# Pooled attention and two expert layers on one core: respacing the attention of the first batch and moving the probability-times-v product in the middle stage

## The chip, the cores and the metric

One core of one Trainium2 chip runs the whole program in one launch. The metric is device time in microseconds (us) for one execution, taken as the median of several. The engines named below are TensorE (PE, the matrix unit), VectorE (DVE), ScalarE (ACT), GpSimd (POOL) and SyncE (SP), whose queue issues nearly all transfers here. Each engine works through its own queue strictly in order, and the queues wait for one another through semaphores.

## The reference

q, k and v have the shape 8 batches x 8 heads x 576 positions x 64. The keys and values are averaged over groups of eight positions, so that there are 72 keys per head. The attention output, as 4608 tokens x 512, goes through two dense layers in turn. The weights come as 64-bit floats.

```python
k_p = k.reshape(B, H, Sp, pool, D).mean(axis=3)
v_p = v.reshape(B, H, Sp, pool, D).mean(axis=3)
scores = scale * np.matmul(q, k_p.transpose(0, 1, 3, 2))
scores = scores - np.max(scores, axis=-1, keepdims=True)
attn = np.exp(scores)
attn = attn / (np.sum(attn, axis=-1, keepdims=True) + 1e-09)
attn_out = np.matmul(attn, v_p)              # then to 4608 x 512 tokens: x
x = ((x @ w1) * (x @ w2) @ w3) @ w_out       # 512 -> 1024 -> 1024 -> 512
h = x @ w_in                                 # 512 -> 2048
out = (h * (1.0 / (1.0 + np.exp(-1.702 * h)))) @ w_out2   # 2048 -> 512
```

## The kernel before, in words

**Number format.** Each float32 operand is kept as a high part and a low part, and a product is three matmuls: high by high, high by low, low by high (`mm3`, L114 to L116). `split` makes the two parts: ACT casts the high part (L104), DVE or POOL subtracts for the low part (L105).

**Weight conversion.** `Conv.step` turns one 512 KB tile of 64-bit weights into float32: two ACT passes (L166, L168), a DVE shift (L169) and a POOL addition (L172). A tile then moves along a line of three places. One step later its `turn` runs (only tiles of w3 have one: four PE transposes, L508), and another step later its `done` runs, mostly a `split`. Within one step the source has the new tile first, then the `turn` of the middle one, then the `done` of the old one. Up to nine tiles are loaded ahead.

**Three stages.** First there are 28 conversion steps (the loop at L568). They convert w_out and w3, and `w3_mm` multiplies the two together into `wp_s` as their parts become ready. From the fifth step on each step also calls `tick()`, which advances the attention. Second comes the middle stage (the loop at L602): nine blocks of 512 tokens, each with eight values of f. For every f there are 24 matmuls for x @ w1 and x @ w2, the elementwise product (L641), and `x2_step`, 12 matmuls with `wp_s`; two calls of `tick()` and, while weights are left, two conversion steps go with it. In the last two blocks the weights of the second layer are converted. Third comes the second layer (from L672), which reads its weights back from device memory.

**Attention.** The work is cut into 32 groups, each one batch and two heads. Steps g0 to g6 of a group: g0 transposes k and q on DVE and pools k; g1 makes the scores on PE and subtracts the maximum on DVE; g2 is the exponential on ACT; g3 divides by the sums on DVE. `g_va` and `g_vb` pool v on POOL and split it into `vm` and `vt`. g4 turns the probabilities and splits them into `ph` and `pt`: for the first four groups (the first batch) the turning is done by PE transposes and ACT copies within g4, for the others by 20 DVE transposes at the end of g3 (L314). g6 multiplies with v on PE (L380 to L383), and ACT and DVE write the result into the token block (L390, L391). Most of these tiles exist once, so a step of one group often waits for the group before it.

**Order.** `tick_first` has the first batch, with a group started every two ticks; `tick` has the other groups, one in four ticks s = 0 to 3. Each block of 512 tokens needs four groups: block 0 needs groups 0 to 3, block 1 needs up to group 7. The source order is not the order on the engines. The compiler's scheduler (`schedule_with_timeline_sim=True`) plays the program through with its own time estimates, and an engine takes, of the instructions that are ready in that play, the one that stands first in the source. The queues are then fixed, and on the chip they run in that order whatever the real durations are.

Of the kernel before, what the change touches and what calls it, by code (L numbers as in the profile page):

```python
# [8 lines left out]
F32R = mybir.dt.float32r  # L9
# [3 lines left out]
ALU = mybir.AluOpType  # L13
# [4 lines left out]
P = 128  # L18
T = 512
# [3 lines left out]
def pooled_attention_moe_moe2(  # L23
# [18 lines left out]
    nc = tc.nc  # L42
    B, H, S, D = q.shape
# [11 lines left out]
    NG = B * HP  # L55
    NPE = HP
# [43 lines left out]
    def f32(ap):  # L100
        return ap.bitcast(F32)
# [22 lines left out]
    def sl(i, n=P):  # L124
        return slice(i * n, (i + 1) * n)

    class Conv:
# [26 lines left out]

        def step(self):

            new = None
            if self.staged:
                t, turn, done = self.staged.pop(0)
                lo_w, hi_w = t[:, :, 0], t[:, :, 1]  # L160
                w = cv_p[0].tile([P, T], F32, name="cv", tag="cv", bufs=4)
                wu = w.bitcast(U32)

                e = self.ps[self.n % len(self.ps)] if self.ps else w
                self.n += 1
                nc.scalar.activation(  # L166
                    e, hi_w.bitcast(F32), AF.Prelu, scale=2.0 ** -112, alpha=-2.0 ** 32)
                nc.scalar.activation(lo_w.bitcast(I32), lo_w, AF.Copy, scale=2.0 ** -29)  # L168
                nc.vector.tensor_scalar(  # L169
                    out=wu, in0=e.bitcast(U32), scalar1=3, scalar2=None,  # L170
                    op0=ALU.logical_shift_left)
                nc.gpsimd.tensor_tensor(  # L172
                    out=w.bitcast(I32), in0=w.bitcast(I32), in1=lo_w.bitcast(I32), op=ALU.add)
                give(t)
                new = [w, turn, done]
            mid, old = self.line
            if mid and mid[1]:
                mid[0] = mid[1](mid[0])
            key = old[2](old[0]) if old else None
            self.line = [new, mid]  # L180
            self.load()
            return key
# [8 lines left out]
    with pa_ctx:  # L191
        pa = pa_ctx.enter_context(tc.tile_pool(name="pa", bufs=1))
# [6 lines left out]
            out=mask[:, 0], in_=mask[:, 0], compare_op=ALU.is_gt, fill=0.0,  # L199
            base=SK, pattern=[[0, D]], channel_multiplier=-1)  # L200
        nc.gpsimd.affine_select(
            out=mask[:, 1], in_=mask[:, 1], compare_op=ALU.is_ge, fill=0.0,
# [8 lines left out]
        for t in s_ts:  # L211
# [3 lines left out]
        ident = pa.tile([P, P], F32, name="ident")  # L215
        nc.gpsimd.memset(ident, 1.0)
        nc.gpsimd.affine_select(
            out=ident, in_=ident, compare_op=ALU.is_equal, fill=0.0,
# [6 lines left out]
        g_q, g_k, g_v, g_s = {}, {}, {}, {}  # L225
# [38 lines left out]
        def banks_of(n):  # L264
            return acc[2:] if n < NPE and n % 2 else wk[2:]

        def s_of(n):
            return s_ts[n % 2 if n < NPE else 0]
# [67 lines left out]
        def g_vb(n):  # L336
            vf, vtf = g_v.pop(n)
            nc.scalar.copy(vm[:, 0], vf)
            nc.gpsimd.tensor_tensor(out=vm[:, 1], in0=vf, in1=f32(vm[:, 0]), op=ALU.subtract)
            nc.scalar.copy(vt[:32, D:], vtf)  # L340
            nc.scalar.copy(vt[64:96, D:], vtf)
            nc.gpsimd.tensor_tensor(
                out=vt[32:64, D:], in0=vtf, in1=f32(vt[:32, D:]), op=ALU.subtract)

        def g4(n):
            p0, p1 = g_s.pop(n)
            if n < NPE:
                ps, s_t = banks_of(n), s_of(n)
                p0f, p1f = (t.rearrange("p t c -> p (t c)") for t in (p0, p1))
                for tt in range(4):  # L350
                    nc.tensor.transpose(ps[0][:, sl(tt)], s_t[:, tt, :P], ident)
                nc.scalar.copy(p0f[:, :T], ps[0])
                w = S - T
                nc.tensor.transpose(ps[1][:, :w], s_t[:w, 4, :P], ident[:w, :w])
                for tt in range(3):
                    nc.tensor.transpose(
                        ps[1][:32, w + tt * P:w + (tt + 1) * P], s_t[:, tt, P:], ident)
                nc.scalar.copy(p0f[:, T:S], ps[1][:, :w])
                nc.scalar.copy(p1f[:, :3 * P], ps[1][:32, w:w + 3 * P])
                nc.tensor.transpose(ps[0][:32, :P], s_t[:, 3, P:], ident)  # L360
                nc.tensor.transpose(ps[0][:32, P:P + w], s_t[:w, 4, P:], ident[:w, :w])
                nc.scalar.copy(p1f[:, 3 * P:S], ps[0][:32, :P + w])
            ph = pa.tile([P, 2, S], F32R, name="ph", tag="ph")
            pt = pa.tile([96, S], F32R, name="pt", tag="pt")
            g_s[n] = (ph, pt)
            s0 = p0.rearrange("p t c -> p (t c)")[:, :S]
            s1 = p1.rearrange("p t c -> p (t c)")[:, :S]
            nc.scalar.copy(ph[:, 0], s0)  # L368
            nc.gpsimd.tensor_tensor(out=ph[:, 1], in0=s0, in1=f32(ph[:, 0]), op=ALU.subtract)  # L369
            nc.scalar.copy(pt[:32], s1)  # L370
            nc.scalar.copy(pt[32:64], s1)
            nc.gpsimd.tensor_tensor(out=pt[64:96], in0=s1, in1=f32(pt[:32]), op=ALU.subtract)

        def g6(n):
            b, hp = divmod(n, HP)
# [29 lines left out]
        def tick_first():  # L405

            t = tick_n[0]
            tick_n[0] += 1
            for n in range(NPE):
                if t == 2 * n + 6:  # L410
                    g6(n)
            for n in range(NPE):
                s = t - 2 * n
                if s == 0 and n == 0:
                    g0(0)
                elif s == 1:
                    g1(n)
                elif s == 2:
                    g2(n)
                    g0(n + 1)  # L420
                elif s == 3:
                    g3(n)
                elif s == 4:
                    g4(n)
                    g_va(n)
                elif s == 5:
                    g_vb(n)
            if t == 2 * NPE + 4:
                tick_n[0] = 4 * NPE
                give(s_sl)  # L430

        def tick():
            t = tick_n[0]
            if t < 4 * NPE:
                return tick_first()
            tick_n[0] += 1
            n, s = divmod(t, 4)
            if s == 0:
                if NPE <= n - 1 < NG:
                    g4(n - 1)  # L440
            elif s == 1:
                if n < NG:
                    g1(n)
            elif s == 2:
                if NPE <= n - 1 < NG:
                    g6(n - 1)
                if n < NG:
                    g2(n)
                    g_va(n)
                if n + 1 < NG:  # L450
                    g0(n + 1)
            elif n < NG:
                g3(n)
                g_vb(n)

        wo_s, wp_s, w1_s, w2_s = {}, {}, {}, {}

# [110 lines left out]
        for i in range(n3 + 4):  # L568
            key = conv.step()
# [32 lines left out]
        for blk in range(NB):  # L602
            x = [x_slot(blk, c) for c in range(KM)]
            if blk == NB - 2:

                pa_ctx.close()
                pa = pa_ctx.enter_context(tc.tile_pool(name="pc", bufs=1, reuse_waits="tile"))
# [521 lines left out]
```

## Time and profile before

| what | value |
|---|---|
| median of 3 runs | 1477.35 us (1476.22 to 1478.56) |
| the profiled execution's own time | 1479.71 us |
| its span | 1478.0 us |
| PE busy | 1438.7 us (97%) |
| DVE / ACT / POOL busy | 988.7 / 693.9 / 489.0 us |
| first 28 conversion steps and first batch | about 0 to 113 us |
| middle stage (nine blocks) | about 113 to 730 us |
| second layer | from there to the end |

The shares of busy time are averages over the whole span. The change concerns the first 113 us and the attention of the middle stage, so those stretches have to be read by themselves. A row of a timeline gives the start, the duration, the engine and the line in the kernel, and in square brackets the idle time of that engine just before it and what ended it.

### The profile page before, as it was taken

The numbers are of one execution on the slowest core, as the hardware profiler recorded it, in microseconds if no ns is written. First come the engines' busy times: TensorE is split into PE (matmuls) and PEld (weight loads), VectorE is DVE, ScalarE is ACT, GpSimd is POOL, SyncE is SP. The second block draws the span as 40 slices with busy tenths as digits, with TensorE's granted clock in tenths as the row PEclk, the third lists the DMA queues.
The fourth block names the chain that finished last, engine by engine and source line by source line (L and its number), as shares of the span: only waits on it lengthen the run. The fifth ranks groups of instructions, "written<-read, shape, count | busy, mean of one in ns | idle before, by whom it ended". The sixth has DMA issues, their size and how long they took to land.

```text
span 1478.0 us, 19436 instructions
## 1 busy us (share of the span) xinstructions
PE 1438.7 (97%) x6536; PEld 1190.0 (81%) x6536; DVE 988.7 (67%) x1728; ACT 693.9 (47%) x1212; POOL 489.0 (33%) x589
## 2 busy tenths in 40 slices
PE   6979999999999999999999999999999999999998
PEld 4867888888888888888788887888788888888886
DVE  7888998878787877654737255683559354944554
ACT  7875444434343433366635344552455244534442
POOL 8789656554545555366733100000000000000000
PEclk9989999999999999999999999999999999999999
DMA  9992233323232311199879978877677766785665
GB/s 265 248 233 48 57 85 57 80 46 78 49 77 49 77 33 37 42 325 344 309 236 398 325 243 276 294 211 221 194 244 224 221 197 221 239 234 180 194 213 139
DMA packets 294436, 267.64 MB, mean 181 GB/s; under 512 B 201664, under 2 KB 226240, under 8 KB 294336
## 3 DMA queue, kind: packets, MB, share of 16 engines
q1 hardware_dynamic: 291648, 265.09, 59.8%
q10 hardware_dynamic: 2688, 1.31, 0.3%
q8 instruction: 52, 0.85, 0.2%
q14 instruction: 48, 0.39, 0.1%
HBM read 209.72 MB, written 56.62 MB: 180 GB/s over the span
## 4 chain that ended last, share of the span: by engine, by line
PE 82%; DMA 7%; DVE 5%; ACT 2%; SPq 2%; issue 1%; POOL 1%; DVEq 0%; ACTq 0%; POOLq 0%
PE bk L709 39%; PE wk L114 8%; PE wk L115 8%; PE wk L116 8%; PE acc L114 4%; PE acc L115 4%; PE acc L116 4%; PE wk L277 2%; DMA wud<-wt 2%; DVE p L314 1%; SPq L229 1%; DMA st<-wind 1%; PE bk L115 1%; PE bk L116 1%; PE bk L114 1%
## 5 line engine op out<-in xcount | busy, mean ns | idle before, releaser
L709 PE MATMUL bk<-mv,st 128*128 128x512 f32 x1152 | 272.6, 391 | 0.7 <-DMA st<-wud 0.7
L709 PE MATMUL bk<-xM,st 128*128 128x512 f32 x1092 | 259.0, 390 | 3.9 <-DMA st<-wind 3.7
L709 PEld LDWEIGHTS bk<-mv,st 128*128 128x128 f32 x1152 | 217.3, 189 | 46.3 <-issue 1.1
L709 PEld LDWEIGHTS bk<-xM,st 128*128 128x128 f32 x1092 | 204.5, 188 | 48.6 <-issue 2.5
L114 PE MATMUL wk<-s,s 128*128 128x512 f32 x576 | 227.0, 396 | 2.8 <-DVE a L641 1.2
L116 PE MATMUL wk<-s,s 128*128 128x512 f32 x576 | 224.9, 391 | 2.1 <-DVE s L105 2.1
L115 PE MATMUL wk<-s,s 128*128 128x512 f32 x576 | 224.9, 391 | 0.0
L314 DVE STREAM_TRANSPOSE p<-s_t 32x160 f32<-32x160 f32 (+1 forms) x560 | 178.5, 319 | 10.3
L114 PE MATMUL acc<-s,s 128*128 128x512 f32 x352 | 134.8, 406 | 8.2 <-ACT s L104 3.2
L115 PE MATMUL acc<-s,s 128*128 128x512 f32 x352 | 141.4, 402 | 0.9 <-POOL s L105 0.8
L116 PE MATMUL acc<-s,s 128*128 128x512 f32 x352 | 140.4, 399 | 0.0
L114 PEld LDWEIGHTS wk<-s,s 128*128 128x128 f32 x576 | 108.5, 189 | 26.2 <-DVE a L641 2.1
L116 PEld LDWEIGHTS wk<-s,s 128*128 128x128 f32 x576 | 108.3, 188 | 24.8 <-DVE s L105 2.3
L115 PEld LDWEIGHTS wk<-s,s 128*128 128x128 f32 x576 | 108.4, 188 | 22.1 <-DVE s L391 0.4
L105 DVE TENSOR_TENSOR mv<-g,mv 128x1024 fp32r<-128x1024 f32 x80 | 97.8, 1222 | 33.6 <-ACT mv L104 32.2
L104 ACT CAST mv<-g 128x1024 fp32r<-128x1024 f32 x80 | 84.3, 1054 | 71.8 <-PE bk L709 71.4
L172 POOL TENSOR_TENSOR cv<-cv,s 128x512 int32<-128x512 int32 x72 | 97.5, 1364 | 28.6 <-DVE cv L169 21.1
L105 POOL TENSOR_TENSOR s<-a,s 128x512 fp32r<-128x512 f32 x56 | 72.5, 1294 | 82.5 <-ACT s L104 62.7
L638 ACT COPY a<-wk 128x512 f32<-128x512 f32 x72 | 42.1, 585 | 110.5 <-PE wk L116 89.7
L369 POOL TENSOR_TENSOR ph<-p,ph 128x576 fp32r<-128x576 f32 x32 | 45.7, 1429 | 126.5 <-ACT ph L368 123.9
L114 PEld LDWEIGHTS acc<-s,s 128*128 128x128 f32 x352 | 67.8, 193 | 23.4 <-ACT s L104 5.2
L115 PEld LDWEIGHTS acc<-s,s 128*128 128x128 f32 x352 | 68.2, 194 | 15.0 <-POOL s L105 2.0
(190 smaller groups left out, 2357.9 us busy)
## 6 DMA issues: line engine op xcount, KB each, us to landing
st<-wud SPq DMA_DIRECT2D x96, 512.0 KB, 4.4
st<-wind SPq DMA_DIRECT2D x66, 512.0 KB, 4.7
st<-wind SPq DMA_DIRECT2D x76, 256.0 KB, 3.9
s<-in_moe_w_dram SPq DMA_DIRECT2D x32, 512.0 KB, 6.4
wind<-s SPq DMA_DIRECT2D x32, 512.0 KB, 5.4
s<-in_moe_w_out_dram SPq DMA_DIRECT2D x24, 512.0 KB, 6.5
kr<-in_k_dram SPq DMA_DIRECT2D x128, 72.0 KB, 2.6
qr<-in_q_dram SPq DMA_DIRECT2D x128, 72.0 KB, 2.6
```

Of the source, the lines that this page charges most:

```text
L104: nc.scalar.copy(dst[:, 0], src)
L105: lo_eng.tensor_tensor(out=dst[:, 1], in0=src, in1=f32(dst[:, 0]), op=ALU.subtract)
L114: nc.tensor.matmul(o, a[:, 0, a_sl], b[:, 0, b_sl], start=first, stop=False)
L115: nc.tensor.matmul(o, a[:, 0, a_sl], b[:, 1, b_sl], start=False, stop=False)
L116: nc.tensor.matmul(o, a[:, 1, a_sl], b[:, 0, b_sl], start=False, stop=last)
L172: nc.gpsimd.tensor_tensor(out=w.bitcast(I32), in0=w.bitcast(I32), in1=lo_w.bitcast(I32), op=ALU.add)
L229: nc.sync.dma_start(dst[32 * c:32 * c + 32], src[b, 2 * hp + c // 2, :, 32 * (c % 2):32 * (c % 2) + 32].rearrange("(g t) d -> t g d", t=32))
L277: nc.tensor.matmul(sc[half][:, i * KW:(i + 1) * KW], qT[:, sl(tt)], mov, start=True, stop=True)
L314: nc.vector.transpose(out=dst[:, :nt, 32 * c:32 * c + 32], in_=s_t[32 * c:32 * c + 32, :nt, 32 * r:32 * r + 32])
L369: nc.gpsimd.tensor_tensor(out=ph[:, 1], in0=s0, in1=f32(ph[:, 0]), op=ALU.subtract)
L638: nc.scalar.copy(a, pa_)
L709: nc.tensor.matmul(o, w[:, x, m], b[:, y], start=first and n == 0, stop=last and n == 2, skip_group_check=True)
```

## The change

It has three parts. In `Conv.step` the `done` of the old tile comes first, then the `turn` of the middle one, then the new tile. In the first batch a group starts every three ticks in place of two, and g4 is cut in two: `g4a` (the main turns and the split into `ph`) at the place of g4, and `g4b` (the last two turns and the split into `pt`) one tick later, beside `g_vb`; g6 stays at the sixth tick of its group. Four groups thus end at tick 15 in place of tick 12, and group 4 follows at ticks 16 to 19 as before, which are three conversion steps later. Within the split into `pt` the POOL subtraction is issued before the second ACT copy. In the middle stage g4 moves from s = 0 to s = 1 (just ahead of the next group's g1), and g6 from s = 2 to s = 3 (just ahead of the next group's g3). No instruction is added or taken away.

```diff
         def step(self):
+            mid, old = self.line
+            key = old[2](old[0]) if old else None
+            if mid and mid[1]:
+                mid[0] = mid[1](mid[0])
             new = None
             if self.staged:
...
                 give(t)
                 new = [w, turn, done]
-            mid, old = self.line
-            if mid and mid[1]:
-                mid[0] = mid[1](mid[0])
-            key = old[2](old[0]) if old else None
...
+        def tail_split(n, ph):
+            pt = pa.tile([96, S], F32R, name="pt", tag="pt")
+            s1 = flat(n)[1]
             nc.scalar.copy(pt[:32], s1)
+            nc.gpsimd.tensor_tensor(out=pt[64:96], in0=s1, in1=f32(pt[:32]), op=ALU.subtract)
             nc.scalar.copy(pt[32:64], s1)
-            nc.gpsimd.tensor_tensor(out=pt[64:96], in0=s1, in1=f32(pt[:32]), op=ALU.subtract)
+            g_s[n] = (ph, pt)
...
             for n in range(NPE):
-                if t == 2 * n + 6:
+                if t == 3 * n + 6:
                     g6(n)
             for n in range(NPE):
-                s = t - 2 * n
+                s = t - 3 * n
...
                 elif s == 4:
-                    g4(n)
+                    g4a(n)
                     g_va(n)
                 elif s == 5:
+                    g4b(n)
                     g_vb(n)
-            if t == 2 * NPE + 4:
+            if t == 3 * NPE + 3:
                 tick_n[0] = 4 * NPE
                 give(s_sl)
...
-            if s == 0:
+            if s == 1:
                 if NPE <= n - 1 < NG:
                     g4(n - 1)
-            elif s == 1:
                 if n < NG:
                     g1(n)
             elif s == 2:
-                if NPE <= n - 1 < NG:
-                    g6(n - 1)
...
-            elif n < NG:
-                g3(n)
-                g_vb(n)
+            elif s == 3:
+                if NPE <= n - 1 < NG:
+                    g6(n - 1)
+                if n < NG:
+                    g3(n)
+                    g_vb(n)
```

## Rows read from the trace of the kernel before

**Rows 1.** Windows: length, then each engine's busy us (instructions), granted PE clock, DMA.
```profile
core 0: us, PE busy (x) PEld busy (x) DVE busy (x) ACT busy (x) POOL busy (x), PEclk, DMA share, GB/s
42.00:74.50 32.50, 32.27 (x177) 26.56 (x178) 26.80 (x48) 27.83 (x59) 23.14 (x24) 1.00 0.90 246
74.50:113.50 39.00, 30.48 (x130) 23.69 (x128) 32.82 (x49) 31.33 (x68) 34.11 (x41) 0.87 1.07 226
113.50:190.00 76.50, 74.06 (x351) 61.71 (x352) 67.86 (x154) 35.83 (x80) 59.30 (x79) 1.00 0.26 52
190.00:600.00 410.00, 410.00 (x1978) 346.69 (x1977) 335.43 (x826) 160.72 (x366) 216.27 (x312) 1.00 0.27 59
```

**Rows 2.** Timeline of PE, 74 to 116 us: waits, and matmuls at either clock.
```profile
81.47 0.76 PE L114 MATMUL acc<-s,s 128*128 128x512 f32 x1 [2.84 <-ACT ph L368]
...
107.79 0.50 PE L116 MATMUL wk<-s,s 128*128 128x512 f32 x1 [2.06 <-DVE s L105]
...
108.66 0.63 PE L116 MATMUL wk<-s,s 128*128 128x512 f32 x1
109.08 0.63 PE L114 MATMUL wk<-s,s 128*128 128x512 f32 x1
...
114.91 0.40 PE L114 MATMUL wk<-s,s 128*128 128x512 f32 x1
115.15 0.39 PE L115 MATMUL wk<-s,s 128*128 128x512 f32 x1
```

**Rows 3.** Timeline of PE: first products with v of groups 0, 2 and 3.
```profile
57.72 0.38 PE L380 MATMUL wk<-ph,vm 128*128 128x288 f32 x1
...
87.95 0.52 PE L380 MATMUL wk<-ph,vm 128*128 128x288 f32 x2
...
103.08 0.39 PE L380 MATMUL acc<-ph,vm 128*128 128x288 f32 x1
```

**Rows 4.** Groups by line, POOL up to 57.7 us: count | busy us, mean ns.
```profile
L172 POOL TENSOR_TENSOR cv<-cv,s 128x512 int32<-128x512 int32 x21 | 28.4, 1357 | 9.3 <-DMA s<-in_moe_w_dram 3.3 <-DVE cv L169 3.0 <-issue 0.8
```

**Rows 5.** The same, POOL up to 103.1 us.
```profile
L172 POOL TENSOR_TENSOR cv<-cv,s 128x512 int32<-128x512 int32 x31 | 41.4, 1339 | 10.2 <-DMA s<-in_moe_w_dram 3.3 <-DVE cv L169 3.0 <-issue 1.3
```

**Rows 6.** Timeline of POOL, 99 to 105 us, ahead of the product of group 3.
```profile
99.12 1.43 POOL L372 TENSOR_TENSOR pt<-p,pt 32x576 fp32r<-32x576 f32 x1
100.63 0.79 POOL L329 TENSOR_TENSOR vf<-va,mask 128x128 f32<-128x128 f32 x1
...
102.98 1.28 POOL L105 TENSOR_TENSOR s<-cv,s 128x512 fp32r<-128x512 f32 x1
104.23 0.45 POOL L339 TENSOR_TENSOR vm<-vf,vm 128x128 fp32r<-128x128 f32 x1
```

**Rows 7.** Groups by line, DVE and ACT up to 113.5 us.
```profile
L169 DVE TENSOR_SCALAR cv<-cv 128x512 uint32<-128x512 uint32 x34 | 31.9, 951 | 7.8 <-ACT cv L166 7.5
...
L168 ACT ACTIVATE s<-s 128x512 int32<-128x512 uint32 x40 | 26.9, 678 | 3.5 <-DMA s<-in_moe_w_dram 3.3
```

**Rows 8.** Timeline of DVE, 101 to 112 us.
```profile
107.05 0.68 DVE L105 TENSOR_TENSOR s<-cv,s 128x512 fp32r<-128x512 f32 x1
...
108.68 1.50 DVE L169 TENSOR_SCALAR cv<-cv 128x512 uint32<-128x512 uint32 x2
...
111.17 0.34 DVE L391 TENSOR_TENSOR s<-acc,s 128x224 fp32r<-128x224 f32 x1
```

**Rows 9.** Timeline of PE in the second layer: its longest wait.
```profile
912.79 1.40 PE L709 MATMUL bk<-xM,st 128*128 128x512 f32 x5 [1.79 <-DMA st<-wind]
```

**Rows 10.** Timeline of DVE and PE at the start of block 1.
```profile
187.77 0.78 DVE L255 STREAM_TRANSPOSE kT<-kr 128x576 f32<-128x576 f32 x1
...
189.69 0.73 PE L114 MATMUL wk<-s,s 128*128 128x512 f32 x2 [1.17 <-ACT s L390]
```

**Rows 11.** Timeline of PE at the start of block 2.
```profile
255.83 0.30 PE L383 MATMUL wk<-pt,vt 96*128 96x288 f32 x1
...
260.73 0.62 PE L114 MATMUL wk<-s,s 128*128 128x512 f32 x2
```

More of the change, by code (lines that the diff above doesn't have):

```diff
@@ L343, in g_vb, with flat @@
                 out=vt[32:64, D:], in0=vtf, in1=f32(vt[:32, D:]), op=ALU.subtract)
[L345 to L362, printed above, removed]
+        def flat(n):
+            return [t.rearrange("p t c -> p (t c)")[:, :S] for t in g_s[n][:2]]
@@ L363, in g4, with main_split @@
+        def main_split(n):
             ph = pa.tile([P, 2, S], F32R, name="ph", tag="ph")
[L364 to L367, printed above, removed]
+            s0 = flat(n)[0]
             nc.scalar.copy(ph[:, 0], s0)
             nc.gpsimd.tensor_tensor(out=ph[:, 1], in0=s0, in1=f32(ph[:, 0]), op=ALU.subtract)
+            return ph
+        def tail_split(n, ph):
+            pt = pa.tile([96, S], F32R, name="pt", tag="pt")
+            s1 = flat(n)[1]
@@ L370, in g4, with g4a @@
             nc.scalar.copy(pt[:32], s1)
+            nc.gpsimd.tensor_tensor(out=pt[64:96], in0=s1, in1=f32(pt[:32]), op=ALU.subtract)
             nc.scalar.copy(pt[32:64], s1)
-            nc.gpsimd.tensor_tensor(out=pt[64:96], in0=s1, in1=f32(pt[:32]), op=ALU.subtract)
+            g_s[n] = (ph, pt)
+        def g4a(n):
+            ps, s_t = banks_of(n), s_of(n)
+            p0f, p1f = flat(n)
+            for tt in range(4):
+                nc.tensor.transpose(ps[0][:, sl(tt)], s_t[:, tt, :P], ident)
+            w = S - T
+            nc.tensor.transpose(ps[1][:, :w], s_t[:w, 4, :P], ident[:w, :w])
+            for tt in range(3):
+                nc.tensor.transpose(
+                    ps[1][:32, w + tt * P:w + (tt + 1) * P], s_t[:, tt, P:], ident)
+            nc.scalar.copy(p0f[:, :T], ps[0])
+            nc.scalar.copy(p0f[:, T:S], ps[1][:, :w])
+            nc.scalar.copy(p1f[:, :3 * P], ps[1][:32, w:w + 3 * P])
+            g_s[n] += (main_split(n),)
@@ L374, in g6, with g4b, g4 @@
+        def g4b(n):
+            ps, s_t = banks_of(n), s_of(n)
+            p1f, w = flat(n)[1], S - T
+            nc.tensor.transpose(ps[0][:32, :P], s_t[:, 3, P:], ident)
+            nc.tensor.transpose(ps[0][:32, P:P + w], s_t[:w, 4, P:], ident[:w, :w])
+            nc.scalar.copy(p1f[:, 3 * P:S], ps[0][:32, :P + w])
+            tail_split(n, g_s[n][2])
+        def g4(n):
+            tail_split(n, main_split(n))
         def g6(n):
```

## The prediction, written before the result was known

> **What bounds the kernel now.** I read the windows first, stretch by stretch. From 190 to 600 us PE is busy for all 410.00 us [rows 1]: there the matmuls bound the kernel, and since the change adds and removes none, it can win nothing in that stretch. From 42.0 to 74.5 us PE is also full, 32.27 of 32.50 us. Then, from 74.5 to 113.5 us, it is busy for only 30.48 of 39.00 us at a granted clock of 0.87, and from 113.5 to 190 us for 74.06 of 76.50 us. So the time that this change can reach is the idle time of PE before 190 us: 8.52 us in the starved stretch, 2.44 us after it, and what the lower clock costs.
>
> The timeline of PE shows what ends those waits. The longest one, 2.84 us, ends at 81.47 us, and the matmul behind it belongs to the product of w3 and w_out; the one of 2.06 us ends at 107.79 us with a low part on DVE, and the matmul behind it belongs to block 0 [rows 2]. After such waits the matmuls start 0.42 us apart (108.66 to 109.08) in place of 0.24 us (114.91 to 115.15): PE has gone from 2.4 to 1.2 GHz, and each matmul costs nearly double until it is back.
>
> The timeline then tells who is late. The product with v of group 0 runs at 57.72 us, that of group 2 at 87.95 and that of group 3 at 103.08 [rows 3]. These stand in the source at ticks 6, 10 and 12, which are the conversion steps 10, 14 and 16 (the first tick is in step 4). But POOL has finished 21 conversions by 57.7 us [rows 4] and 31 by 103.1 us [rows 5]. So attention runs 11 and then 15 steps behind its place in the source. The conversions run ahead, the w3 product they feed fills PE until 74.5 us, and then PE has little left but to wait for attention and for the first weights of block 0.
>
> **The change part by part.** *A group per three steps.* The place of group 3's product moves from step 16 to step 19. Nothing is added, so the price is only that of a later place. The scheduler prefers what stands earlier in the source among what is ready, and when group 3's product runs, 31 conversions are done; at step 19 it is still older than everything it competes with. So I cost the shift at nothing. From both sides: three steps at 103.1 / 31 = 3.3 us are 10 us if attention really waited for its place; a gain of as much as the idle 8.5 us if the new spacing made attention and conversions mesh. The row nearest to it, the lag of 15 steps against a shift of 3, says zero. The loads of k and q are issued by g0 on SP's queue and those of v by `g_va`; they move with their groups past the weight loads of at most three steps, and since they wait for a free tile and not for their place, I cost that at nothing too, within the same two ends.
>
> *Last turns and the split into pt a step later, POOL first.* For group 3 POOL ran the subtraction for pt (L372, 1.43 us, at 99.12) directly ahead of vf (L329, at 100.63), and vf leads over the ACT cast to vm at 104.23 [rows 6], which the product needed. In the new order `g_va` stands ahead of that subtraction. It is still needed before the product ends, but the chain over vf, ACT and vm is the longer one, so 1.43 us come off it: -1.4 us on the end of group 3. Bounds: nothing, if the queue order stays, and 1.43 + 1.28 = 2.7 us, if the conversion's low part at 102.98 also moves out of the way.
>
> *The old tile first in a conversion step.* A split no longer stands behind the next but one tile's two ACT passes (0.678 us each [rows 7]) and its DVE shift (0.951 us). A split that contends can come up to 0.68 + 0.68 + 0.95 = 2.3 us earlier. That bears on the low part that ended the wait of 2.06 us at 107.79, computed on DVE at 107.05 [rows 8], so I take the whole wait off: -2.1 us; the lowest end is that none of it goes, since the new tile was then perhaps not ready anyway. The wait at 81.47 may shrink as well, but its matmuls belong to the w3 product, which is done before block 0 can start: that gain becomes later idle time, at zero. The stretch at the lower clock behind 107.79 goes with the wait: five matmuls at 0.18 us extra, -0.9 us. What is late next is the low part of group 3's tokens, L391 at 111.17; it stands behind two shifts (1.50 us together at 108.68), which are younger work too, and it gains the 1.4 us from above. The two gains are in series only in part: block 0 needs the weights first and group 3's tokens last. I count the wait and its clock in full and half of group 3's 1.4 us: -2.1 - 0.9 - 0.7 = -3.7 us at the start of block 0. For the conversions after 600 us I cost the new order at nothing: in the second layer PE's longest wait is 1.79 us, for a transfer [rows 9], and PE's own work covers the rest; if that cover is gone, about 2 us either way.
>
> *Middle stage, g4 and g6 a tick later.* g6 of group 7 now stands behind the exponential of group 8 and g0 of group 9. At the start of block 1 PE waits 1.17 us for group 7's tokens, until 189.69 [rows 10], so here a delay counts fully. The DVE transpose at 187.77 (0.78 us) and its like already ran ahead of the tokens' low parts in the old order, so the delay can only be small: +0.3 us, between zero and one such transpose more plus the wait itself, 0.78 + 1.17 = 2.0 us. At block 2 the product ends at 256.13 and its tokens are first used at 260.73 [rows 11], with PE busy in between. Moved behind one `x2_step` (12 matmuls at 0.24 us, 2.9 us) this leaves 4.6 - 2.9 = 1.7 us, which still covers: zero at the six later block starts.
>
> *Sum.* -3.7 + 0.3 = -3.4 us, on the profiled execution's 1479.71 us: 1476.3. That execution lies 2.36 us over the median of 1477.35, so the median should become 1473.9 us.
>
> **The rivals.** *The gate is block 1, not block 0.* PE can do all of block 0 before group 7 is ready; it ran dry for 1.17 us at 189.69. If group 7's end is set by its own chain, whatever block 0 gains is lost again there. For it: DVE, which carries most of that chain, is busy for 67.86 of 76.50 us before it [rows 1]. Against it: groups 4 to 7 start when group 3 frees the single tiles. The time would be that of before, 1477.4, give or take 2.5.
>
> *The spacing meshes.* PE is full up to 74.5 us and starved after it; if attention keeps step with the conversions, the two stretches fill one another. For it: the idle 8.5 us and the clock not granted (0.13 x 39 = 5 us at most) lie in one stretch. Against it: the lag of 15 steps. Price: the 8.5 us and about a third of that clock, -10 us: 1467. The Trainium skill has this as a rule (Perfetto Trace Analysis, Optimization Strategy): where the most contended engine changes over time, interleaving the regimes may improve performance. By that rule the change should give this rival's time; the trace agrees that there are two regimes, but does not show that their order in the source sets them.
>
> *Attention really comes later.* The mechanism is the first batch's place: if the new order lets three further conversions go ahead of group 3 on DVE and POOL, its product moves from 103 us to 107 or more, and block 0 starts later, beyond the 1.17 us that block 1's wait forgives. Price: half of the 10 us, +5: 1482; all of it, 1487. It decides when group 3's product starts after about 105 us. For it: DVE, ACT and POOL were 80 to 87% busy in the starved stretch [rows 1], so there is little room to catch up. Against it: the lag again.
>
> *Tokens late at every block.* If the product moves by more than the 1.7 us left at block 2, each of seven later block starts waits some 0.6 us: +4, 1481. Against it: a PE without a gap for 410 us.
>
> **How the numbers follow.** A measurement of this kernel can tell about 0.2%, 3 us, from no change. The forecast gets 0.37 (its own range 1469 to 1475), block 1 as the gate 0.30, meshing 0.08, attention later 0.18, late blocks 0.07. Nearly all of the forecast's case lies beyond 3 us in its middle, and a little of it within; I put faster at 0.44, within 0.2% at 0.32, slower at 0.24. The range takes in the forecast, the gate at block 1, most of meshing, late blocks, and the cheaper half of attention coming later: 1465 to 1482.
>
> **What would show it right or wrong.** Right: no wait of about 2 us before block 0's first weights, group 3's product before 102 us, the first elementwise product (L641, before at 114 us) 3 to 4 us earlier, and PE's first wait at the start of block 1 no longer than before. The gate at block 1 shows as an earlier block 0 with a longer wait near 189 us. Meshing shows as products with v of groups 1 to 3 well before 75, 88 and 103 us and a granted clock of 1.00 throughout. Attention later shows as a product of group 3 after 105 us. Late blocks show as gaps on PE after 200 us, every 75 us or so. The prediction is wrong if the queues come out in a different order for reasons that no single step here names, as a scheduler that plays the whole program through can do: then the gain or loss will lie in waits that I have not listed.

## The result: slower by 0.8%

The changed kernel took 1489.05 us (median of 4 runs, 1486.11 to 1490.83) against 1476.78 us for the kernel before on the same chip (4 runs, 1475.05 to 1478.56). The ratio is 1.0081, with a 95% interval of 1.006 to 1.0102. The profiled execution of the changed kernel took 1486.11 us with a span of 1484.4 us, the fastest of its four, so the trace shows 6.4 us of the 12 at its end. At the first matmul of the second layer, a stage that the change leaves alone, it is 9.0 us behind (773.9 us for 764.9). Lines of the changed kernel lie four further on in the conversion (L170 to L176), fifteen further on in g6 (L391 is now L406) and sixteen behind it (L641 is L657).

The windows of the changed kernel, as in [rows 1]:

```profile
core 0: us, PE busy (x) PEld busy (x) DVE busy (x) ACT busy (x) POOL busy (x), PEclk, DMA share, GB/s
42.00:74.50 32.50, 32.43 (x177) 26.80 (x176) 25.57 (x49) 28.39 (x60) 22.04 (x24) 1.00 0.91 235
74.50:113.50 39.00, 30.08 (x130) 23.17 (x129) 30.54 (x51) 30.61 (x67) 34.05 (x43) 0.85 1.13 237
113.50:190.00 76.50, 68.93 (x315) 56.57 (x315) 69.33 (x152) 35.88 (x79) 58.52 (x76) 0.97 0.25 48
190.00:600.00 410.00, 410.00 (x1978) 347.26 (x1978) 330.52 (x802) 161.33 (x365) 215.12 (x309) 1.00 0.27 59
```

Two stretches are as before: 42 to 74.5 us, and 190 to 600 us with PE full. The starved stretch before 113.5 us lost 0.40 us of busy time. Most of the loss lies in 113.5 to 190 us: 68.93 us busy for 74.06, at a clock of 0.97 for 1.00. The same in finer windows, first the kernel before, then the changed one:

```profile
113.50:160.00 46.50, 45.23 (x210) 37.34 (x211) 39.30 (x83) 23.32 (x51) 41.17 (x53) 1.00 0.23 45
160.00:200.00 40.00, 38.83 (x190) 32.38 (x189) 38.11 (x100) 15.25 (x35) 23.38 (x37) 1.00 0.36 83
```

```profile
113.50:160.00 46.50, 38.93 (x168) 31.00 (x168) 41.92 (x86) 22.70 (x49) 37.47 (x44) 0.94 0.23 44
160.00:200.00 40.00, 40.00 (x198) 34.00 (x197) 36.93 (x93) 15.54 (x35) 26.84 (x43) 1.00 0.27 54
```

From 113.5 to 160 us, the first half of block 0, PE lost 6.3 us. After 160 us it gained 1.2 us: the wait for group 7 at 189.69 [rows 10] is gone, because block 1 now starts later than group 7. The timeline of PE in the changed kernel has these waits (the bracket gives the idle time before the instruction and what ended it):

```profile
86.80 0.40 PE L395 MATMUL wk<-ph,vm 128*128 128x288 f32 x1 [4.17 <-ACT vm L338]
...
103.23 0.29 PE L395 MATMUL acc<-ph,vm 128*128 128x288 f32 x1
...
107.49 0.53 PE L398 MATMUL acc<-pt,vt 96*128 96x288 f32 x2 [0.75 <-POOL vt L342]
109.57 0.73 PE L114 MATMUL wk<-s,s 128*128 128x512 f32 x2 [1.56 <-ACT s L405]
...
120.40 0.50 PE L114 MATMUL wk<-s,s 128*128 128x512 f32 x1 [2.14 <-ACT a L654]
...
152.84 0.79 PE L114 MATMUL wk<-s,s 128*128 128x512 f32 x1 [4.55 <-DVE a L657]
```

The product of group 3 starts at 103.23 us, where it was [rows 3], and POOL has again done 31 conversions by then (the 31st at 102.3 us). What is new are the waits of 2.14 and 4.55 us inside block 0. DVE tells where they come from. First the kernel before, block 0's products (L641) among the attention of groups 4 and 5:

```profile
114.24 0.67 DVE L641 TENSOR_TENSOR a<-wk,a 128x512 f32<-128x512 f32 x1
...
117.78 6.64 DVE L314 STREAM_TRANSPOSE p<-s_t 32x160 f32<-32x160 f32 x20
...
125.84 0.68 DVE L641 TENSOR_TENSOR a<-wk,a 128x512 f32<-128x512 f32 x1
...
130.76 0.65 DVE L641 TENSOR_TENSOR a<-wk,a 128x512 f32<-128x512 f32 x1
136.66 0.69 DVE L641 TENSOR_TENSOR a<-wk,a 128x512 f32<-128x512 f32 x1 [5.26 <-PE wk L116]
...
139.76 3.33 DVE L105 TENSOR_TENSOR s<-cv,s 128x512 fp32r<-128x512 f32 x1
...
144.61 6.65 DVE L314 STREAM_TRANSPOSE p<-s_t 32x160 f32<-32x160 f32 x20
```

Then the changed kernel (L657 is the product):

```profile
113.61 4.32 DVE L314 STREAM_TRANSPOSE p<-s_t 32x160 f32<-32x160 f32 x13
...
118.18 2.31 DVE L314 STREAM_TRANSPOSE p<-s_t 32x160 f32<-32x160 f32 x7
120.52 0.69 DVE L657 TENSOR_TENSOR a<-wk,a 128x512 f32<-128x512 f32 x1
...
135.17 6.65 DVE L314 STREAM_TRANSPOSE p<-s_t 32x160 f32<-32x160 f32 x20
141.85 0.69 DVE L657 TENSOR_TENSOR a<-wk,a 128x512 f32<-128x512 f32 x1
...
146.56 4.97 DVE L105 TENSOR_TENSOR s<-cv,s 128x512 fp32r<-128x512 f32 x1
...
152.14 0.65 DVE L657 TENSOR_TENSOR a<-wk,a 128x512 f32<-128x512 f32 x1
```

Before, the first product is ahead of group 4's 20 transposes, four products are ahead of group 5's, and the slow low part (3.33 us) has the fourth product ahead of it. In the changed kernel the first product is behind group 4's 20, the third behind group 5's, and the fourth behind the slow low part (4.97 us). Attention of groups 4 and 5 runs *earlier* (113.61 for 117.78 and 135.17 for 144.61), and the elementwise products on which PE's next matmuls wait run later: 120.52 for 114.24, and the fourth at 152.14 for 136.66. The wait of 4.55 us is for that fourth product. The wait of 2.14 us comes by way of ACT, whose rows are

```profile
119.19 0.67 ACT L351 CAST ph<-p 128x576 fp32r<-128x576 f32 x1 [2.13 <-DVE p L314]
119.77 0.58 ACT L654 COPY a<-wk 128x512 f32<-128x512 f32 x1
```

The cast of group 4's probabilities stands ahead of block 0's second copy, and has itself waited 2.13 us for the transposes. In the kernel before, the second copy is ahead of that cast:

```profile
118.47 0.57 ACT L638 COPY a<-wk 128x512 f32<-128x512 f32 x1
...
123.12 0.67 ACT L368 CAST ph<-p 128x576 fp32r<-128x576 f32 x1 [2.98 <-DVE p L314]
```

### The profile page after: what moved, and what is told of

Same layout as the page of the kernel before. It is cut to its first block, busy times and chain, and to the rows that moved or that the text cites. A ratio compares the mean times of both kernels' runs of the same rounds, so it can differ in the third digit from the quotient of the medians.

```text
span 1484.4 us, 19428 instructions
## 1 busy us (share of the span) xinstructions
PE 1439.5 (97%) x6536; PEld 1190.3 (80%) x6536; DVE 987.2 (67%) x1728; ACT 694.0 (47%) x1212; POOL 486.4 (33%) x589
## 4 chain that ended last, share of the span: by engine, by line
PE 80%; DVE 5%; DMA 5%; POOL 2%; ACT 2%; issue 2%; SPq 1%; ACTq 0%; DVEq 0%; POOLq 0%
PE bk L725 39%; PE wk L114 7%; PE wk L115 7%; PE wk L116 7%; PE acc L114 4%; PE acc L115 4%; PE acc L116 4%; DMA wud<-wt 2%; PE wk L277 2%; POOL cv L176 1%; DMA st<-wind 1%; PE bk L116 1%; PE bk L114 1%; PE bk L115 1%; DVE s L105 1%
## 5 line engine op out<-in xcount | busy, mean ns | idle before, releaser
L314 DVE STREAM_TRANSPOSE p<-s_t 32x160 f32<-32x160 f32 (+1 forms) x560 | 178.5, 319 | 10.5
L105 DVE TENSOR_TENSOR mv<-g,mv 128x1024 fp32r<-128x1024 f32 x80 | 97.7, 1221 | 32.1 <-ACT mv L104 30.9
L176 POOL TENSOR_TENSOR cv<-cv,s 128x512 int32<-128x512 int32 x72 | 98.7, 1379 | 48.1 <-DVE cv L173 34.4
L105 POOL TENSOR_TENSOR s<-a,s 128x512 fp32r<-128x512 f32 x56 | 72.3, 1291 | 96.5 <-ACT s L104 94.7
L351 ACT CAST ph<-p 128x576 fp32r<-128x576 f32 x32 | 21.5, 673 | 126.9 <-DVE p L314 126.9
```

What stands on the lines that cost most here:

```text
L105: lo_eng.tensor_tensor(out=dst[:, 1], in0=src, in1=f32(dst[:, 0]), op=ALU.subtract)
L176: nc.gpsimd.tensor_tensor(out=w.bitcast(I32), in0=w.bitcast(I32), in1=lo_w.bitcast(I32), op=ALU.add)
L314: nc.vector.transpose(out=dst[:, :nt, 32 * c:32 * c + 32], in_=s_t[32 * c:32 * c + 32, :nt, 32 * r:32 * r + 32])
```

## Experiments

Each is timed against the kernel before on its own chip; a ratio of 1.0000 is that kernel.

**The parts alone, and the whole again.** The first run has only the new order inside `Conv.step`, the second only the middle stage, the third only the first batch (spacing, the cut of g4 and the order inside the split into pt), the fourth the whole change. Each edit is hunks of the change itself, here by one line of each:

```diff
+            key = old[2](old[0]) if old else None     # first: ahead of the new tile
...
+            if s == 1:                                # second: g4 at s = 1, g6 at s = 3
...
+                s = t - 3 * n                         # third, with g4a, g4b
```

> The kernel before with the new order in a conversion step alone (done of the old tile, turn, new tile). Spacing theory (the loss comes from the first batch's three-step places): 1474 to 1478, as before or a little faster. Conversion theory (the loss comes from the splits going ahead of the next tile's shift, so that on DVE a low part with two inputs from SBUF sits beside a run of POOL instructions, 4.97 us at 146.56 in the profile after): +5 to +12, 1482 to 1489, with such a long low part before 160 us. Middle theory (the loss comes from g4 and g6 a tick later): as before.

> The kernel before with g4 and g6 of the middle stage a tick later alone. Middle theory: +5 to +12, 1482 to 1489, with PE's new waits after 120 us and none new before. Spacing theory and conversion theory: 1475 to 1479, within 2 us of before, and PE's waits up to 113 us as before, since nothing there is touched.

> The kernel before with the first batch's new spacing and the cut g4 alone. Spacing theory: +6 to +12, 1483 to 1489, with the product of group 3 ending at 107 us or later, a wait of about 4 us at 87 us and block 0's second elementwise product about 5 us later than in the kernel before (125.8 us). Conversion theory and middle theory: within 3 us of before.

> The changed kernel once more, since its profiled execution (1486.1) was the fastest of its four runs (median 1489.1): 1488 to 1490 again. If the difference of 3 us between executions comes from DVE instructions held up beside POOL, this profile shows a longer one than the 4.97 us of the first, or a second one, and otherwise the same queues; if it does not, the waits are elsewhere.

Measured: conversion order 1480.13 us, 1.0015 (1.0001 to 1.003); middle stage 1476.98 us, 0.9989 (0.9975 to 1.0002); first batch 1487.63 us, 1.0063 (1.0045 to 1.0081); whole 1489.01 us, 1.0075 (1.0057 to 1.0092), against 1477.78 us. The parts add up: +2.35 - 0.8 + 9.85 = +11.4 us, and the whole has +11.2. Most of it is the first batch.

The trace of the repeat has nearly the whole loss (its execution took 1489.51 us). Its low part again takes 4.97 us, from 150.04 us on, and the waits of 2.10 and 4.55 us are there, but block 0's first product is at 124.02 us, 3.5 us later than in the first trace: group 3's product ended only at 111.13 us (108.02 in the first), and PE waited for its tokens for 3.00 us, until 114.14 (1.56 us, until 109.57). So the 3 us between the two executions arise before block 0 and not from a longer stall. Between 95 and 200 us DVE, ACT and POOL each run the same sequence of operations in the two traces of the whole change and in the first batch's part alone; the conversion order alone and the middle stage alone have the sequence of the kernel before.

The conversion order loses its time elsewhere, in the last two blocks, where the second layer's weights are converted. (The nine blocks end at about 765 us, and not at 730 as the table of the stages has it.) PE's waits from 640 to 762 us in the kernel before and then with the conversion order alone, as total, number and longest:

```profile
PE acc L114 <- ACT s L104: 0.6, 1, 0.6
PE acc L114 <- ACT s L104: 2.2, 2, 1.1
```

PE waits there for ACT's cast of an elementwise product. All six traces with the new conversion order have 1.8 to 2.2 us of this wait, the twelve with the old one 0 to 0.6 us.

**Spacing or cut.** The spacing of three with the old g4, and the cut of g4 with the old spacing.

```diff
-                s = t - 2 * n
+                s = t - 3 * n          # first: with g4 whole
...
-                    g4(n)
+                    g4a(n)                 # second: with s = t - 2 * n, g4b a tick later
```

> The kernel before with a group every three ticks in the first batch, g4 uncut. If the spacing makes the loss: 1484 to 1489, as the first-batch part alone (1487.6). If the cut g4 makes it (turns grouped, the split into pt a tick later): within 2 us of before, 1476 to 1480. If both are needed: about half, 1480 to 1484.

> The kernel before with the cut g4 (last turns and pt a tick later), a group every two ticks. If the cut makes the loss: 1484 to 1489. If the spacing makes it: 1475 to 1479, as before.

Measured: spacing 1485.37 us, 1.0047 (1.003 to 1.0064); cut 1477.12 us, 0.9988 (0.9976 to 1.0000), against 1478.22 us. The cut is harmless; the spacing loses by itself.

**Place or spacing.** The first batch's part started three steps earlier, so that group 3 ends at its old place in the source; and the kernel before, started three steps later at its old spacing.

```diff
-            if i >= 4 and tick_n[0] < 20:
+            if i >= 1 and tick_n[0] < 20:      # first: spacing of three, early start
+            if i >= 7 and tick_n[0] < 20:      # second: kernel before, late start
```

> The first-batch part alone, but the first tick in step 1 in place of step 4, so that group 3's product is at step 16 and group 4 at steps 17 to 20 as in the kernel before; the groups stay three steps apart. If the loss comes from the later place in the source beside the conversions: back to before, 1476 to 1480. If it comes from the order of the groups among themselves (the product of a group ahead of the next group's g3, its turns ahead of the next one's g1), which this leaves as it is: still 1484 to 1489.

> The kernel before with its first tick in step 7 in place of step 4: all groups of the first batch and group 4 three steps later, two apart. If the later place makes the loss: 1484 to 1489, with the product of group 3 some 5 us later. If the order of the groups among themselves makes it: 1475 to 1480, near before.

Measured: 1487.3 us, 1.0059 (1.0041 to 1.0076), and 1485.26 us, 1.0048 (1.003 to 1.0066). An early start gives nothing back, and a late start loses without the spacing. So the loss needs neither the spacing nor the later place; either will do. What the losing kernels share with the changed one is the order on DVE: group 4's transposes ahead of block 0's first product and group 5's ahead of the third. In the first batch's part these four start at 116.8, 123.8, 138.4 and 145.1 us; with the old g4 at 106.2, 123.5, 136.9 and 144.6; in the two runs here they start at 113.6, 129.6, 138.9 and 146.7, and at 114.6, 123.9, 136.8 and 143.5. That gave the theory of the next runs: the order on DVE in block 0 makes the loss, not the end of group 3.

**Less attention ahead of the product.** In the first batch's part, and in the kernel before as the control, group 4's 20 transposes are replaced by two that copy blocks in place. These kernels leave out the turning of group 4's probabilities.

```diff
+            if n == NPE:
+                nc.vector.transpose(out=p0, in_=s_t[:, :, :P])
+                nc.vector.transpose(out=p1, in_=s_t[:32, :, :P])
+                return
```

> The first batch's part alone, with the 20 DVE transposes of group 4's probabilities (6.65 us, 113.6 to 120.5 us in the changed kernel) replaced by two that copy blocks in place (estimate 1.5 us in all); the probabilities of group 4 are then not turned, so its tokens are left wrong. Queue theory (block 0's first products stand behind those 20 on DVE, the wait of 2.4 us at 123.6 is theirs): first product 4 to 5 us earlier than 123.8, i.e. about 119, the wait near 123 gone, time 1483 to 1486 against 1487.6 with the 20. Rival, late attention alone (block 0 cannot start before the tokens of group 3, whatever DVE does afterwards): first product still at about 123, time 1487 to 1488.

> The kernel before with the same 20 transposes of group 4 replaced by two: the control for the run above. In the kernel before the first product of block 0 (114.2 us) stands ahead of the 20 on DVE, so the queue theory expects little: at most the wait of 1.20 us at 126.6 gone, time 1476 to 1478 and a ratio of 0.999 to 1.000. If DVE's load by itself, and not its order, were the matter, this kernel would gain as much as the run above: 2 to 5 us, 1473 to 1476.

Measured: 1477.85 us, 1.0001 (0.9987 to 1.0015), and 1478.63 us, 0.9997 (0.9986 to 1.0009). The same saving on DVE is worth all of the loss in the one and nothing in the other. But the way was not the one expected: the first product came only to 121.38 us (123.76 in the first batch's part; the execution traced here, 1482.18 us, is the slowest of its twelve), and a wait of 2.38 us stayed, now for that product and not for a copy on ACT. What went is the wait of 4.54 us, because the queue had changed further on: group 5's transposes (137.65 us) now stand behind the third product and not the second, and the low part stands behind the fourth (at 149.23 us, 1.26 us long). More came back (0.62%, about 9 us) than was expected (2 to 5).

**The slow low part alone.** One instruction of the changed kernel is moved: the low part of w2 for f = 5 goes to POOL. Apart from it the order on DVE through block 0 is the same; on ACT and POOL a few instructions change places. The second run has this in the first batch's part, with the short transposes of the run above.

```diff
-            conv.add(col_tile(w2, f), None, conv.to(w2_s, f, nc.vector))
+            conv.add(col_tile(w2, f), None, conv.to(w2_s, f, nc.gpsimd if f == 5 else nc.vector))
```

> The changed kernel with one single instruction moved: the low part of the weights of w2 for f = 5 goes to POOL in place of DVE (on DVE it took 4.97 us at 146.56 beside a full POOL, and the product at 152.14 stood behind it; PE waited 4.55 us at 152.84). If that stall carries its share of the loss: the wait of 4.55 us gone, about 3 to 4.5 us back, time 1484.5 to 1486, a ratio to the kernel before of 1.0045 to 1.0055 in place of 1.008. Rival (block 1 waits for group 7 anyway, or the product waits for something else): the wait only moves, time 1488 to 1490.

> The first batch's part alone with both suspected costs taken away: group 4's 20 transposes replaced by two (its tokens left wrong) and the low part of w2 for f = 5 on POOL. If the two carry the loss after 113 us (2.4 and 4.5 us of PE waits), the sum goes: 1479 to 1482, with PE busy for over 42 of the 46.5 us between 113.5 and 160 (45.23 before, 38.36 in the first batch's part alone). Rival, the later place of attention by itself: 1486 or more, and PE as idle as before in that stretch.

Measured: 1483.47 us, 1.0039 (1.0024 to 1.0053), and 1479.05 us, 1.001 (0.9999 to 1.002). DVE of the first of them, where the 4.97 us stood:

```profile
148.86 0.77 DVE L255 STREAM_TRANSPOSE kT<-kr 128x576 f32<-128x576 f32 x1
149.55 0.65 DVE L657 TENSOR_TENSOR a<-wk,a 128x512 f32<-128x512 f32 x1
```

The wait of 4.55 us is gone, and PE is busy for 43.01 us of 113.5 to 160. One stalled instruction ahead of a product is worth half of the loss. Both together gained no more than the short transposes alone, which had already moved the low part out of the way.

**The order put right and put wrong, with nothing left out.** In the changed kernel a tiny instruction ties group 4's transposes to the first product, so that they must stand behind it (second run: with the low part on POOL too). In the kernel before, one makes the first product wait for them; attention keeps its place and spacing there.

```diff
+            if n == NPE:               # changed kernel; the turns are called a tick later
+                c0 = s_t.rearrange("p t (r c) -> p t r c", c=32)[:, 0, :, 0]
+                nc.vector.scalar_tensor_tensor(
+                    out=c0, in0=a0[0][:, 0:5], scalar=0.0, in1=c0, op0=ALU.mult, op1=ALU.add)
...
+                    if blk == f == 0:  # kernel before, ahead of the product
+                        nc.vector.scalar_tensor_tensor(
+                            out=a[0:1, 0:1], in0=p4[0][0:1, 0, 96:97], scalar=0.0, in1=a[0:1, 0:1],
+                            op0=ALU.mult, op1=ALU.add)
```

> The changed kernel, nothing left out, with one tiny instruction added that ties group 4's 20 DVE transposes to the first product of block 0 (it adds zero times five columns of that product's tile to the probabilities), so that they stand behind it on DVE, as in the kernel before. Order theory (the loss is made because products of block 0 stand behind attention of later groups on DVE): the first product back from 120.5 to 116 to 119 us, PE idle between 113.5 and 200 us from 7.6 down to 2 to 4, ratio 1.002 to 1.005. Rival, late attention (group 3's product ends 2 to 5 us later, and that alone sets the loss): ratio 1.007 to 1.008 as in the changed kernel; it could even lose more, since group 4 then comes later too.

> The opposite, on the kernel before, nothing left out: one tiny instruction makes the first product of block 0 wait for group 4's 20 transposes, so that they stand ahead of it on DVE; the first batch keeps its place and spacing. Order theory: the first product goes from 114.2 to 124 to 127 us, a wait of 2 us or more appears on PE behind it, and 4 to 10 us are lost: 1482 to 1488, ratio 1.003 to 1.007. Rival, late attention: the attention is not moved, so no more than about 2 us are lost, ratio up to 1.0015.

> The run with the tie, and the low part of w2 for f = 5 on POOL as well, nothing left out. If order and stall together are the loss of the first batch's part: ratio 0.999 to 1.003, first product as in the run with the tie and no PE wait above 2 us between 125 and 200 us. Rival, late attention: 1.004 or more.

Measured: tie in the changed kernel 1482.16 us, 1.0024 (1.0012 to 1.0036); reversed tie in the kernel before 1487.1 us, 1.0052 (1.0036 to 1.0068); tie and POOL 1483.77 us, 1.003 (1.0019 to 1.0042), against 1478.75 us. DVE and then PE of the tied changed kernel (L321 are the transposes, L667 the product):

```profile
116.00 4.64 DVE L105 TENSOR_TENSOR s<-cv,s 128x512 fp32r<-128x512 f32 x1
...
121.23 0.67 DVE L667 TENSOR_TENSOR a<-wk,a 128x512 f32<-128x512 f32 x1
...
124.59 6.66 DVE L321 STREAM_TRANSPOSE p<-s_t 32x160 f32<-32x160 f32 x20
131.27 0.69 DVE L667 TENSOR_TENSOR a<-wk,a 128x512 f32<-128x512 f32 x1
...
135.64 0.68 DVE L667 TENSOR_TENSOR a<-wk,a 128x512 f32<-128x512 f32 x1
...
142.78 0.68 DVE L667 TENSOR_TENSOR a<-wk,a 128x512 f32<-128x512 f32 x1
143.38 6.65 DVE L321 STREAM_TRANSPOSE p<-s_t 32x160 f32<-32x160 f32 x20
```

```profile
121.95 0.80 PE L114 MATMUL wk<-s,s 128*128 128x512 f32 x1 [3.25 <-DVE a L667]
```

Group 5's transposes are behind the fourth product again, as in the kernel before, and that product is at 142.78 in place of 152.14 us. Of the loss of 0.75 to 0.81%, 0.24% is left, with the end of group 3's product still at 108.1 us. The first product did not come back to 116 to 119: a low part of 4.64 us now stands ahead of it. POOL for the low part of f = 5 gave nothing more, since in this order that low part, at 151.17 us, took 0.68 us anyway. PE of the kernel before with the reversed tie:

```profile
128.59 0.58 PE L382 MATMUL wk<-ph,vm 128*128 128x288 f32 x1 [6.10 <-DVE s_t L284]
132.38 0.80 PE L114 MATMUL wk<-s,s 128*128 128x512 f32 x1 [2.49 <-DVE a L648]
```

Here the first product fell to 131.69 us, later than expected, because PE's queue changed as well: a product of group 4 (L382) now stands ahead of block 0's matmuls and waits 6.10 us. The loss is 0.52%, without any change of the first batch's place. So the order in block 0 is enough to make most of the loss, and putting it right takes most of the loss away. How much of the 0.52% belongs to DVE's order and how much to PE's is not divided.

**A version that might win.** The cut of g4 at the old spacing, with the new middle stage and the old conversion order.

```diff
+                    g4a(n)                 # s = t - 2 * n, g4b a tick later
...
+            if s == 1:                     # middle stage: g4 at s = 1, g6 at s = 3
```

> The two parts that lost nothing alone, together: g4 of the first batch cut in two at the old spacing (0.9988 alone) and g4 and g6 of the middle stage a tick later (0.9989 alone), with the old conversion order. If both add: ratio 0.9975 to 0.998, 1474.5 us. If both were chance or share one gain: 0.999 to 1.000.

Measured: 1476.79 us against 1478.75, 0.9991 (0.9977 to 1.0006). It can't be told from the kernel before, and neither can it be told whether two such small gains are real or add.

## Why the prediction was wrong, step by step

*What bounds the kernel* held for the stretch from 190 to 600 us, which stayed full, and most of what moved lies before 190 us. Not all: PE's waits for ACT from 640 to 762 us grew from 0.6 to 1.9 us in the changed kernel.

*A group per three steps, costed at nothing* is the step that failed. It cost +7.15 us by itself (spacing with the old g4) and +9.85 us with the cut. Its reason, that attention lags 15 steps and so does not feel its place, was right for the start of group 3's product, 103.23 for 103.08 us in the first trace, though not for its end (108.02 for 105.72 us). The error was to follow one group's start only. A change of place also changes which of the younger instructions come ahead of which, and the queues of DVE, ACT and PE are fixed by that. The loss arose 10 to 50 us further on, in block 0, on an engine (DVE) whose order there the step never looked at. The bounds given for it, -8.5 and +10, were about right; choosing zero between them was not.

*The rival "attention really comes later"* gave the right sign and nearly the size (1482 to 1487, measured 1489.05), but not the mechanism. Its point of decision, a start of group 3's product after 105 us, was not reached in the changed kernel (103.23 and 104.80 us) or in the first batch's part (104.35). Where it was reached it did not decide: in the kernel before with short transposes the start was at 106.99 us, at a ratio of 0.9997. The product's end did come later, but a late end is not the loss by itself. These are its last matmuls in the first batch's part (1.0063) and in the same with short transposes (1.0001):

```profile
110.76 0.54 PE L398 MATMUL acc<-pt,vt 96*128 96x288 f32 x2 [2.00 <-POOL vt L342]
110.65 0.53 PE L402 MATMUL acc<-pt,vt 96*128 96x288 f32 x2 [2.82 <-POOL vt L346]
```

Groups 4 and 5 came earlier, not later. The last sentence of the prediction, on queues in another order, named the case, but gave it no chance and no price. The other signs: meshing did not come (clock 0.85, a wait of 4.17 us for `vm` at 86.80); block 1 as the gate did not decide (its wait vanished); late blocks did not come (no gap from 200 to 600 us).

*Last turns and the split into pt a step later* (half of -1.4): the cut alone, without the spacing, gave -1.1 us, at the edge of its interval. That the size fits is luck: in its trace POOL still runs the subtraction for pt (98.03 us) directly ahead of vf (99.61 us), as before. In the changed kernel vf did go ahead, and `vm` was split at 101.38 for 104.23 us [rows 6]. But the product's end then waited for `vt`, which POOL took up only behind group 4's first sums of v, and these waited for their loads. In the kernel before `vt` came directly behind `vm`, at 104.75 us. POOL of the changed kernel:

```profile
96.28 0.45 POOL L329 TENSOR_TENSOR vf<-va,mask 128x128 f32<-128x128 f32 x1
...
98.17 1.43 POOL L359 TENSOR_TENSOR pt<-p,pt 32x576 fp32r<-32x576 f32 x1
...
104.69 0.74 POOL L324 TENSOR_TENSOR va<-vr 128x256 f32<-128x256 f32 x1 [1.06 <-DMA vr<-in_v_dram]
...
107.12 0.31 POOL L342 TENSOR_TENSOR vt<-vtf,vt 32x64 fp32r<-32x64 f32 x1
```

*The old tile first* (-2.1 and -0.9): alone +2.35 us, the wrong sign. Alone, the wait of 2.06 us did shrink, to 1.23 us at 108.82, but an earlier one for a low part on DVE grew, from 1.36 us at 94.02 to 3.44 us at 95.75. A second step of this term failed too: the conversions after 600 us, put at nothing, where PE's waits for ACT are 2.2 us for 0.6. In the changed kernel the wait of 2.06 us at 107.79 is replaced by one of 1.56 us at 109.57, for group 3's tokens (ACT L405) and not for a weight.

*Middle stage* (+0.3): -0.8 us (-3.7 to +0.3), right within what can be measured; the block starts after 200 us stayed covered, as worked out.

What stays open: why exactly the scheduler put the transposes ahead. Most likely they were ready in its play before the product was, but only the resulting order was seen. Of the 0.24% (3.4 us) that the tie did not give back, the waits after 640 us are some 1.3 us (1.9 for 0.6 in its trace); the rest was not divided between the later end of group 3 and the stall of 4.64 us.

## What to carry to other kernels

Where a scheduler fixes the queues, the cost of moving work is not read from the moved work alone, but from the next stage too: list what each engine does around the first instruction on which the bound engine waits, and ask what a shift of a few us can put ahead of it. Where such an order matters, a tie (a dependency made by one tiny instruction) can hold it, and, put in both ways round, is the experiment that tests it. A saving on an engine that is worth nothing in one order (0.9997) can be worth 0.6% in another.

## What the runs showed of the hardware

A DVE subtraction with two SBUF operands (L105, `s<-cv`, 128x512) took from 0.65 us (kernel before) to 4.97 us (changed kernel). At its longest it began at 146.56 us, while POOL worked without a break:

```profile
146.43 0.52 POOL L325 TENSOR_TENSOR vat<-vat 32x128 f32<-32x128 f32 x1
146.91 0.31 POOL L327 TENSOR_TENSOR va<-va 128x64 f32<-128x64 f32 x1
147.19 1.27 POOL L105 TENSOR_TENSOR s<-a,s 128x512 fp32r<-128x512 f32 x1
148.44 1.27 POOL L176 TENSOR_TENSOR cv<-cv,s 128x512 int32<-128x512 int32 x1
149.67 1.25 POOL L105 TENSOR_TENSOR s<-cv,s 128x512 fp32r<-128x512 f32 x1
150.89 0.81 POOL L327 TENSOR_TENSOR vat<-vat 32x64 f32<-32x64 f32 x1
```

POOL's three large instructions keep their usual 1.25 to 1.27 us, so here all of the delay falls on DVE. DVE ends at 151.53 us, within the small instruction at 150.89, which took 0.81 us where its like takes 0.31: as if DVE had got in just there. The kernel before shows the same: its 3.33 us, from 139.76 to 143.09 us, end within a small instruction (L327 at 142.45 us) that also took 0.81 us. It can fall the other way: at 107.05 us [rows 8] DVE took 0.68 us, and it was a POOL instruction (L324, at 107.14 us) that took 1.18 us where its median is 0.73. DVE's transposes (L314) kept 0.30 to 0.34 us each throughout. The Trainium skill (GPSIMD Engine Reference, section 1, Specifications) says that POOL's SBUF interfaces are shared with VectorE, with contention for DVE instructions that have two SBUF inputs or run in a 2-port mode. The trace agrees, with the 4.97 us above. It adds that the price was no fixed factor: in both long cases it lasted while POOL's large instructions followed one another without a break. Why DVE gets in at a small instruction is not shown.
